# The order of TensorE work by the size of the weight loads in an attention and feed-forward kernel

## The chip, the cores and the metric

The kernel runs on one core of one Trainium2 chip. The metric is the device time of one execution in microseconds (us). The kernel before the change takes 1217.96 us (median of three runs, 1214.26 to 1219.36).

## What is computed

Eight batches of eight heads of causal attention over 576 tokens of width 64, with a forget gate whose cumulated logarithm is added to the scores, and then a layer norm, a two-layer feed-forward block (512 to 2048 to 512) and a residual over the 4608 tokens:

```
scores = scale * np.matmul(q, k.transpose(0, 1, 3, 2))
cum = np.cumsum(np.log(np.clip(f, 0.0001, 1.0)), axis=-1)
scores = np.where(causal, -1e9, scores + cum[:, :, :, None] - cum[:, :, None, :])
attn = np.exp(scores - np.max(scores, axis=-1, keepdims=True))
attn = attn / (np.sum(attn, axis=-1, keepdims=True) + 1e-09)
x = np.matmul(attn, v)            # heads side by side: (8, 576, 512)
xn = (x - mu) / np.sqrt(var + 1e-06) * g_ln
out = x + np.maximum(xn @ w_ch1, 0.0) @ w_ch2
```

All of it is held to the accuracy of float32, though TensorE multiplies in a shorter format: a factor is split into a high part and a low part (a rounded copy and what the rounding lost), and the products of high by high, high by low and low by high are added up in PSUM.

## The kernel before, in words

**Slots.** The program is one stream of slots, numbered u. A slot stands for a pair (head n, row tile t), t = 1 to 4; 64 heads make 256 slots. A row tile has 128 queries, and the tile t needs the keys up to its diagonal: 192, 320, 448 and 576. The first 64 queries of a head are a small tile t = 0 of 64 queries by 64 keys, done in the slot of t = 1. Keys are cut into one block of 64 and blocks of 128.

**What a slot issues.** The string in the table ORDERS that is valid for the slot says in which order its pieces are issued; each letter is one piece. The strings change at u = 37 and u = 66. The letters that matter here:

- Q: scores of (n, t) on TensorE (qk_mm, lines 374, 376 and 377), a product of the high parts and one of the rest;
- S, e, B: the softmax of the same tile: minimum and mask on VectorE (L409), exponential on ScalarE (L420), the reciprocal on VectorE (L425, L426), the scaling on GpSimd (L427) and a DMA on SyncE's queue (L440) that copies the tile p to pw, a tile with TensorE's short type;
- t: transposes on TensorE of the tile that was made two slots earlier (transpose_unit, recorded at L446 for pw and L448 for p);
- h, l: their results are copied from PSUM by ScalarE (L504, the high part ph) and subtracted by VectorE (L509, the low part pl);
- A: the product with v (av_unit, L543), in slots of t = 1 and t = 3 alone, for the rows transposed in the slots before;
- F, a: its result is copied by ScalarE (L579) and added by VectorE (L590), and sent to memory (L592);
- M, r, m: twelve products of the feed-forward's first layer (L622 to L624) and the two parts of their result, by ScalarE (L630) and VectorE (L635);
- N: six products of the second layer (L644 to L646) for the result of the slot before.

So after u = 66 a slot is a few small products of the attention followed by twelve products of 256 columns and six of 512 columns of the feed-forward. Each engine executes what it is given in the order of issue. The PSUM banks of all these pieces are one ring of six (tag b).

**Two kinds of heads.** Heads 0 to 15 (h.full) are computed in float32 throughout, while the feed-forward's weights are prepared; their products with v (L518) write the two halves of the columns to different partitions. Heads 16 to 63 use the short type and the split parts.

**Stationary and moving.** A product on TensorE first loads its stationary operand (PEld in the profile: LDWEIGHTS), and then streams the moving one. In the profile's form "128\*64 128x256" the stationary operand has 128 rows and 64 columns, and 256 columns are streamed. A transpose has the data as its stationary operand and streams the 128 columns of an identity; the transpose of a 64-key block has a stationary operand of 64 columns, all others have 128. The scores of tile t = 0 have 64 columns, as have the low parts of the product with v (pl times the high half of v); the high parts have 128.

Of the kernel before, what the change touches and what calls it, by code (L numbers as in the profile page):

```python
# [17 lines left out]
P = 128  # L18
# [30 lines left out]
ORDERS = [  # L49
    (0, "WwQsSthAeMrgFBmlLNPaRf"),  # L50
    (37, "WwQSstAMhPelgNFrfmBDLRba"),
    (66, "QSAFteahBlMPrmNbRLD"),
]


# [1 line left out]
def attn_moe(ctx: ExitStack, tc: tile.TileContext, qk, v, f, g, w1, w2, out):  # L57
# [385 lines left out]
    def tr(out_, in_):  # L443
        m = in_.shape[0]
        if in_.dtype == F32R:
            nc.tensor.transpose(out_.bitcast(F32R), in_, identr[:m, :m])  # L446
        else:
            nc.tensor.transpose(out_, in_, ident[:m, :m])  # L448
# [5 lines left out]
    def transpose_unit(h, t):  # L454
        n = f"{h.n}"
        pt = h.p[t][0]
        work_ = []
        if t <= 2:
            if t == 1:
                if h.full:  # L460
                    h.ph1 = padded_keys("ph1", 704, S1)
                else:
                    h.ph1 = work.tile([P, 704], F32R, tag="ph1", bufs=1, name=f"ph1_{n}")
                h.pl1 = None if h.full else pools["late"].tile([P, 384], F32R, tag="pl1", bufs=1, name=f"pl1_{n}")
            ph = h.ph1
            pl = ph if h.full else h.pl1
            tp = bank(f"tr{n}_{t}")
            if t == 1:
                tr(tp[0:64, 0:128], h.p[0][0])
                tr(tp[0:64, 64:192], pt[:, 0:64])  # L470
                tr(tp[:, 192:320], pt[:, 64:192])
                work_.append((tp[0:64, 0:192], ph[0:64, 0:192], ph[64:128, 0:192]))
                work_.append((tp[:, 192:320], ph[:, 320:448], pl[:, 0:128]))
            else:
                tr(tp[0:64, 0:128], pt[:, 0:64])
                tr(tp[:, 128:256], pt[:, 64:192])
                tr(tp[:, 256:384], pt[:, 192:320])
                work_.append((tp[0:64, 0:128], ph[0:64, 192:320], ph[64:128, 192:320]))
                work_.append((tp[:, 128:384], ph[:, 448:704], pl[:, 128:384]))
        else:  # L480
            if t == 3:
                if h.full:
                    h.ph2 = padded_keys("ph2", 9 * P, S - S1)
                else:
                    h.ph2 = work.tile([P, 9 * P], F32R, tag="ph2", bufs=1, name=f"ph2_{n}")
                h.pl2 = None if h.full else pools["late"].tile([P, 7 * P], F32R, tag="pl2", bufs=1, name=f"pl2_{n}")
            c = 0 if t == 3 else P
            ph = h.ph2[:, : 8 * P].rearrange("p (k c) -> p k c", k=4)[:, :, c : c + P]
            pl = None if h.full else h.pl2[:, : 6 * P].rearrange("p (k c) -> p k c", k=3)[:, :, c : c + P]
            tp = bank(f"tr{n}_{t}").rearrange("p (k c) -> p k c", k=4)  # L490
            tr(tp[0:64, 0, :], pt[:, 0:64])
            for k in range(1, 4):
                tr(tp[:, k, :], pt[:, 64 + P * (k - 1) : 64 + P * k])
            work_.append((tp[0:64, 0, :], ph[0:64, 0, :], ph[64:128, 0, :]))
            work_.append((tp[:, 1:4, :], ph[:, 1:4, :], pl))
            if t == 4:
                tp = bank(f"tr{n}_4b")[:, :P]
                tr(tp, pt[:, 64 + 3 * P : 64 + 4 * P])
                work_.append((tp, h.ph2[:, 8 * P :], None if h.full else h.pl2[:, 6 * P :]))
        h.parts = work_  # L500

    def transposed_hi(h, t):
# [8 lines left out]
    def av_unit(h, t):  # L511
        po = bank(f"o{h.n}_{t}")

        if h.full:

            def fac(cols, k, mv, first=False):
                half = slice(0, 64) if cols.start < SPLIT[t] else slice(64, P)
                mm(po[half, cols], h.vr[:, k], mv, start=first, stop=True, skip_group_check=True)  # L518

            if t == 2:  # L520
                ph = h.ph1
                for k, c0, q0 in ((0, 0, 0), (1, 320, 64)):
                    fac(slice(q0, 192), k, ph[:, c0 : c0 + 192 - q0], k == 0)
                    fac(slice(192, 320), k, ph[:, c0 + 192 - q0 : c0 + 320 - q0], k == 0)
                fac(slice(192, 320), 2, ph[:, 576:704])
                h.o = (po, S1, 0)
            else:
                ph = h.ph2
                for k in range(4):
                    for i in range(2):  # L530
                        c0 = 256 * k + P * i
                        fac(slice(P * i, P * i + P), k, ph[:, c0 : c0 + P], k == 0)
                fac(slice(128, 256), 4, ph[:, 8 * P :])
                h.o = (po, S - S1, S1)
            return

        vv = h.vv

        def both(k):
            return vv[:, k].rearrange("p a d -> p (a d)")  # L540

        def acc(o, st, mv, first=False):
            mm(o, st, mv, start=first, stop=True, skip_group_check=True)  # L543

        if t == 2:
            ph, pl, w, c0 = h.ph1, h.pl1, S1, 0
            acc(po[:, 0:320], both(0), ph[:, 0:320], True)
            acc(po[:, 64:320], both(1), ph[:, 320:576])
            acc(po[:, 192:320], both(2), ph[:, 576:704])
            acc(po[0:64, 64:320], vv[:, 1, 0, :], pl[:, 0:256])  # L550
            acc(po[0:64, 192:320], vv[:, 2, 0, :], pl[:, 256:384])
        else:
            ph, pl, w, c0 = h.ph2, h.pl2, S - S1, S1
            for k in range(4):
                acc(po[:, 0:256], both(k), ph[:, 256 * k : 256 * k + 256], k == 0)
            acc(po[:, 128:256], both(4), ph[:, 8 * P :])
            for k in range(1, 4):
                acc(po[0:64, 0:256], vv[:, k, 0, :], pl[:, 256 * (k - 1) : 256 * k])
            acc(po[0:64, 128:256], vv[:, 4, 0, :], pl[:, 6 * P :])
        h.o = (po, w, c0)  # L560

    xs_tile = {}
# [246 lines left out]
    for u, slot in enumerate(slots):  # L809
# [4 lines left out]
        if slot is not None:  # L814
            n, t = slot
            h = hd[n]
# [2 lines left out]
            av = hd[before(LAG + 1)[0]]  # L819
        want = moe.can(wp.ready()) and u >= FIRST_MOE  # L820

        def piece(c):
            tu = before(LAG)
            if c == "t" and tu is not None:
                transpose_unit(hd[tu[0]], tu[1])
            elif c == "h" and tu is not None:
                transposed_hi(hd[tu[0]], tu[1])
            elif c == "l" and tu is not None:
                transposed_lo(hd[tu[0]])
            elif c == "Q" and slot is not None:  # L830
                if t == 1:
                    qk_mm(h, 0)
                qk_mm(h, t)
            elif c == "A" and av is not None:
                av_unit(av, before(LAG + 1)[1])
            elif c == "S" and slot is not None:
                if t == 1:
                    softmax_a(h, 0)
                softmax_a(h, t)
            elif c == "e" and slot is not None:  # L840
                if t == 1:
                    softmax_e(h, 0)
                softmax_e(h, t)
            elif c in FILL:
                wp.fill(FILL[c])
            elif c == "s":
                wp.sums()
                if u == LAG:
                    busy(WARM[2])
            elif c == "F" and av is not None:  # L850
                finish(av)
            elif c == "a" and av is not None:
                finish_add(av)
            elif c == "r" and want:
                moe.first_high()
            elif c == "R":
                moe.limit = min(NCHUNK, max(0, u - LAG - 1) // (4 * H) * S // C)
                moe.rest()
            elif c == "b":
                rows_stats(moe.cur)  # L860
            elif c == "L":
                run_later(RSTD)
            elif c == "M" and want:
                moe.first()
            elif c == "B" and slot is not None:
                if t == 1:
                    softmax_b(h, 0)
                softmax_b(h, t)
            elif c == "m" and want:
                moe.first_low()  # L870
            elif c == "W":
                due = 1 + min(u, W_CHANGE) / W_SLOTS + max(0, u - W_CHANGE) * W_TICKS
                while not wp.done() and wp.tick_no <= due:
                    wp.tick()
            elif c == "N":
                moe.second()
            elif c == "P":
                prep()
            elif c == "D":
                next_raw()  # L880
# [81 lines left out]
```

## Time and profile before

| what | value |
|---|---|
| median of three runs | 1217.96 us (1214.26 to 1219.36) |
| the profiled execution's own time | 1217.98 us |
| its span, first to last instruction | 1216.1 us |
| transposes of pw, 128 columns (L446), 432 | mean record 240 ns |
| transposes of pw, 64 columns (L446), 240 | mean record 226 ns |
| product with v, low part, 256 moving columns (L543), 192 | mean record 279 ns |
| weight load of 128 columns for a product of the feed-forward (L622) | mean record 191 ns |
| weight load of 128 columns for a transpose (L446) | mean record 141 ns |
| weight load of 64 columns for a transpose (L446) | mean record 111 ns |

A record of a matmul or a weight load is longer than the time until the next one starts, since they are pipelined. So durations can't be added up here; what can be added up are the distances between the starts of successive records.

### The profile page before, as it was taken

Reading aid. Unit: us, or ns where it says so; the run is one execution under the profiler, and the core shown is the slowest. Engines: PE = TensorE matmul, PEld = TensorE weight load, DVE = VectorE, ACT = ScalarE, POOL = GpSimd, SP = SyncE. Lnnn points to the kernel's source line nnn. Section 1 sums busy time; section 2 is a strip of 40 time slices with the busy share of each in tenths; the row PEclk is TensorE's granted clock in tenths of the full one; section 3 lists DMA queues with packets and bytes.
Section 4 is the critical chain, followed back from the end, with each engine's and each line's share of the span. In section 5 each row is a group of like instructions: output and inputs, shape, how many; then the busy total and the mean of one; then the engine's idle time right before and its main releaser. Section 6 shows DMA issues by size and latency. Waiting matters only on the chain.

```text
span 1216.1 us, 25716 instructions
## 1 busy us (share of the span) xinstructions
PE 1190.1 (98%) x8368; PEld 1068.3 (88%) x8368; DVE 757.0 (62%) x2664; ACT 619.3 (51%) x1936; POOL 452.6 (37%) x768
## 2 busy tenths in 40 slices
PE   8888998999999999999999999999999999999998
PEld 6557887899999989999999999999999999999997
DVE  6777683477777767777767676767677752222122
ACT  6886574555555555555555555556555541112111
POOL 3543344454444434454534344445444410000000
PEclk9998998999999999999999999999999999999999
DMA  6454452243434344434344444434444421111100
GB/s 192 142 153 151 127 148 63 87 133 131 139 125 143 123 141 131 146 129 135 124 129 141 129 135 131 143 120 139 132 132 131 128 86 41 31 36 39 31 26 27
DMA packets 127541, 139.00 MB, mean 114 GB/s; under 512 B 32432, under 2 KB 100016, under 8 KB 127408
## 3 DMA queue, kind: packets, MB, share of 16 engines
q1 hardware_dynamic: 127408, 137.36, 36.6%
q8 instruction: 67, 1.10, 0.4%
q14 instruction: 66, 0.54, 0.1%
HBM read 79.61 MB, written 19.17 MB: 81 GB/s over the span
## 4 chain that ended last, share of the span: by engine, by line
PE 91%; DVE 3%; ACT 2%; DMA 1%; issue 1%; POOL 1%; SPq 0%; DVEq 0%; ACTq 0%; POOLq 0%
PE h L622 12%; PE h L624 11%; PE h L623 11%; PE acc L644 11%; PE acc L645 11%; PE acc L646 11%; PE o L543 6%; PE tr L446 4%; PE s L376 3%; PE s L377 3%; PE s L374 2%; PE o L518 2%; PE tr L448 1%; ACT p L420 1%; DVE p L409 1%
## 5 line engine op out<-in xcount | busy, mean ns | idle before, releaser
L427 POOL TENSOR_SCALAR p<-p,st 64x64 f32<-64x64 f32 (+4 forms) x320 | 169.9, 532 | 511.5 <-ACT ph L504 232.4
L622 PE MATMUL h<-x,w1h 128*128 128x256 f32 x1152 | 342.3, 297 | 0.4 <-DVE st L409 0.4
L624 PE MATMUL h<-x,w1l 128*128 128x256 f32 x1152 | 326.8, 284 | 0.0
L623 PE MATMUL h<-x,w1h 128*128 128x256 f32 x1152 | 326.3, 283 | 0.0
L420 ACT ACTIVATE p<-p,st 64x64 f32<-64x64 f32 (+4 forms) x320 | 179.2, 561 | 210.6 <-DVE st L409 206.0
L635 DVE SCALAR_TENSOR_TENSOR hh<-h,hh 128x256 fp32r<-128x256 f32 x288 | 120.5, 418 | 194.4 <-ACT hh L630 192.0
L644 PE MATMUL acc<-w2h,hh 128*128 128x512 f32 x576 | 228.4, 397 | 0.0
L645 PE MATMUL acc<-w2l,hh 128*128 128x512 f32 x576 | 227.8, 396 | 0.0
L646 PE MATMUL acc<-w2h,hh 128*128 128x512 f32 x576 | 225.5, 391 | 0.0
L622 PEld LDWEIGHTS h<-x,w1h 128*128 128x128 f32 x1152 | 219.6, 191 | 5.3 <-issue 0.9
L623 PEld LDWEIGHTS h<-x,w1h 128*128 128x128 f32 x1152 | 220.6, 192 | 2.5
L624 PEld LDWEIGHTS h<-x,w1l 128*128 128x128 f32 x1152 | 220.3, 191 | 0.0
L630 ACT ACTIVATE hh<-h 128x256 fp32r<-128x256 f32 x288 | 109.9, 381 | 184.5 <-PE h L624 184.2
L409 DVE CUSTOM_DVE_ANT_0 p<-s,mask 64x64 f32<-64x64 f32 (+4 forms) x320 | 132.2, 421 | 26.4 <-PE s L377 17.7
L646 PEld LDWEIGHTS acc<-w2h,hh 128*128 128x128 f32 x576 | 108.5, 188 | 24.7
L425 DVE TENSOR_SCALAR st<-st 128x1 f32<-128x1 f32 (+1 forms) x320 | 47.7, 149 | 120.2 <-ACT p L420 117.2
L644 PEld LDWEIGHTS acc<-w2h,hh 128*128 128x128 f32 x576 | 109.5, 190 | 14.0 <-ACT ph_full L504 0.2
L645 PEld LDWEIGHTS acc<-w2l,hh 128*128 128x128 f32 x576 | 109.5, 190 | 11.7
L504 ACT CAST ph<-tr 64x128 fp32r<-64x128 f32 (+4 forms) x384 | 107.2, 328 | 3.6 <-PE tr L446 1.3
L579 ACT COPY ot<-o 64x320 f32<-64x320 f32 x96 | 38.0, 396 | 125.5 <-PE tr L446 63.7
L509 DVE TENSOR_TENSOR pl<-tr,ph 128x128 fp32r<-128x128 f32 x192 | 88.0, 458 | 4.3
L377 PE MATMUL s<-kl,xq 66*128 66x288 f32 (+4 forms) x288 | 83.2, 297 | 0.0
(89 smaller groups left out, 1888.7 us busy)
## 6 DMA issues: line engine op xcount, KB each, us to landing
raw<-in_qk_dram SPq DMA_DIRECT2D x96, 288.0 KB
wr<-in_w_dram SPq DMA_DIRECT2D x32, 512.0 KB
pw<-p SPq DMA_DIRECT2D x48, 288.0 KB
pw<-p SPq DMA_DIRECT2D x48, 224.0 KB
vr<-in_v_dram SPq DMA_DIRECT2D x64, 160.0 KB
out_dram<-xt SPq DMA_DIRECT2D x36, 256.0 KB
pw<-p SPq DMA_DIRECT2D x48, 160.0 KB
xa<-xs SPq DMA_DIRECT2D x32, 160.0 KB
```

The costliest lines, as they stand in the source:

```text
L377: mm(sp, xq, kl, start=False, stop=True)
L409: nc.vector.tensor_tensor_reduce(out=pt[:m, a:z], in0=sp, in1=mask[:m, off + a : off + z], scale=-SCALE, scalar=3.0e38 if i == 0 else st[: ...
L420: nc.scalar.activation(pt[:m, :w], pt[:m, :w], AF.Exp, bias=st[:m, i : i + 1], scale=-1.0, accum_out=st[:m, 2:3])
L427: nc.gpsimd.tensor_scalar(out=pt[:m, :w], in0=pt[:m, :w], scalar1=st[:m, 3:4], scalar2=1.0, op0=ALU.mult, op1=ALU.mult)
L622: mm(ph, w1h[:, k, fs], c.x[k][:, 0, :], start=(k == 0), stop=False)
L623: mm(ph, w1h[:, k, fs], c.x[k][:, 1, :], start=False, stop=False)
L624: mm(ph, w1l[:, k, fs], c.x[k][:, 0, :], start=False, stop=(k == KT - 1))
L630: nc.scalar.activation(h[:, 0, :], c.ph, AF.Relu)
L635: nc.vector.scalar_tensor_tensor(out=h[:, 1, :], in0=ph, scalar=0.0, in1=h[:, 0, :].bitcast(F32), op0=ALU.max, op1=ALU.subtract)
L644: mm(c.acc[i], h[:, 0, ts_], w2h[:, j, :], start=(j == 0), stop=False)
L645: mm(c.acc[i], h[:, 0, ts_], w2l[:, j, :], start=False, stop=False)
L646: mm(c.acc[i], h[:, 1, ts_], w2h[:, j, :], start=False, stop=(j == FT - 1))
```

## The change

The instructions are the same, and the data. Their order changes in four ways:

1. In every row of transposes, the transpose of the 64-key block (for t = 1 also that of the tile t = 0) is issued last.
2. From u = 66 on, the transposes t stand ahead of the product with v, A. In the same string the exponential e and the reciprocal and scaling B now stand ahead of F, a.
3. In the product with v of heads 16 to 63, the low part of 128 moving columns is issued ahead of those of 256.
4. In slots of t = 1 of heads 16 to 63, the tile t = 1 comes ahead of the tile t = 0 in Q, S, e and B.

```
 ORDERS = [
     (0, "WwQsSthAeMrgFBmlLNPaRf"),
     (37, "WwQSstAMhPelgNFrfmBDLRba"),
-    (66, "QSAFteahBlMPrmNbRLD"),
+    (66, "QStAeBFahlMPrmNbRLD"),
 ]
...
             if t == 1:
+                tr(tp[:, 192:320], pt[:, 64:192])
                 tr(tp[0:64, 0:128], h.p[0][0])
                 tr(tp[0:64, 64:192], pt[:, 0:64])
-                tr(tp[:, 192:320], pt[:, 64:192])
...
             else:
-                tr(tp[0:64, 0:128], pt[:, 0:64])
                 tr(tp[:, 128:256], pt[:, 64:192])
                 tr(tp[:, 256:384], pt[:, 192:320])
+                tr(tp[0:64, 0:128], pt[:, 0:64])
...
-            tr(tp[0:64, 0, :], pt[:, 0:64])
             for k in range(1, 4):
                 tr(tp[:, k, :], pt[:, 64 + P * (k - 1) : 64 + P * k])
...
             if t == 4:
-                tp = bank(f"tr{n}_4b")[:, :P]
-                tr(tp, pt[:, 64 + 3 * P : 64 + 4 * P])
...
+                tb = bank(f"tr{n}_4b")[:, :P]
+                tr(tb, pt[:, 64 + 3 * P : 64 + 4 * P])
...
+            tr(tp[0:64, 0, :], pt[:, 0:64])
...
             acc(po[:, 192:320], both(2), ph[:, 576:704])
+            acc(po[0:64, 192:320], vv[:, 2, 0, :], pl[:, 256:384])
             acc(po[0:64, 64:320], vv[:, 1, 0, :], pl[:, 0:256])
-            acc(po[0:64, 192:320], vv[:, 2, 0, :], pl[:, 256:384])
...
             acc(po[:, 128:256], both(4), ph[:, 8 * P :])
+            acc(po[0:64, 128:256], vv[:, 4, 0, :], pl[:, 6 * P :])
             for k in range(1, 4):
                 acc(po[0:64, 0:256], vv[:, k, 0, :], pl[:, 256 * (k - 1) : 256 * k])
-            acc(po[0:64, 128:256], vv[:, 4, 0, :], pl[:, 6 * P :])
...
+        def tiles(h, t):
+            if t > 1:
+                return [t]
+            return [0, 1] if h.full else [1, 0]
...
             elif c == "Q" and slot is not None:
-                if t == 1:
-                    qk_mm(h, 0)
-                qk_mm(h, t)
+                for i in tiles(h, t):
+                    qk_mm(h, i)
```

The pieces S, e and B are changed as Q is.

The first place is TensorE in the slot of t = 1 of head 37, from its scores to the first product of the feed-forward (s: scores, o: product with v, tr: transposes, h: feed-forward). Before:

```order
L376 MATMUL s_0_0_8083<-hi_7951 64x128
L377 MATMUL s_0_0_8083<-kl_7952,xq_2933 64x128
L376 MATMUL s_1_0_8086<-hi_7951 128x192
L377 MATMUL s_1_0_8086<-kl_7952,xq_2933 128x192
L543 MATMUL o_2_8094<-ph_36_7985,vv_8019 128x320
L543 MATMUL o_2_8094<-ph_36_7985,vv_8019 128x256
L543 MATMUL o_2_8094<-ph_36_7985,vv_8019 128x128
L543 MATMUL o_2_8094<-pl_36_7986,vv_8019 64x256
L543 MATMUL o_2_8094<-pl_36_7986,vv_8019 64x128
L446 MATMUL tr_3_8105<-identr,pw_3_7999 64x128
L446 MATMUL tr_3_8105<-identr,pw_3_7999 128x128 x3
L622 MATMUL h_8_8126<-x_0_7148,w1h 128x256
```

And with the change, at the same place on TensorE:

```order
L376 MATMUL s_1_0_8083<-hi_7951 128x192
L377 MATMUL s_1_0_8083<-kl_7952,xq_2933 128x192
L376 MATMUL s_0_0_8086<-hi_7951 64x128
L377 MATMUL s_0_0_8086<-kl_7952,xq_2933 64x128
L446 MATMUL tr_3_8096<-identr,pw_3_7993 128x128 x3
L446 MATMUL tr_3_8096<-identr,pw_3_7993 64x128
L543 MATMUL o_2_8101<-ph_36_7973,vv_8019 128x320
L543 MATMUL o_2_8101<-ph_36_7973,vv_8019 128x256
L543 MATMUL o_2_8101<-ph_36_7973,vv_8019 128x128
L543 MATMUL o_2_8101<-pl_36_7974,vv_8019 64x128
L543 MATMUL o_2_8101<-pl_36_7974,vv_8019 64x256
L622 MATMUL h_8_8126<-x_0_7148,w1h 128x256
```

The first number of a row's size is here that of the stationary operand's columns. The pair of scores of 64 columns has moved behind that of 128, the transposes ahead of the product, and in both groups the one of 64 columns and 128 moving ones has changed its place.

The second place is TensorE in the slot of t = 3 of the same head. Before:

```order
L377 MATMUL s_3_0_8214<-kl_7952,xq_2933 128x448
L543 MATMUL o_4_8220<-ph_36_8103,vv_8019 128x256 x4
L543 MATMUL o_4_8220<-ph_36_8103,vv_8019 128x128
L543 MATMUL o_4_8220<-pl_36_8104,vv_8019 64x256 x3
L543 MATMUL o_4_8220<-pl_36_8104,vv_8019 64x128
L446 MATMUL tr_1_8235<-identr,pw_2893 64x128
L446 MATMUL tr_1_8235<-identr,pw_1_8122 64x128
L446 MATMUL tr_1_8235<-identr,pw_1_8122 128x128
```

And with the change:

```order
L377 MATMUL s_3_0_8214<-kl_7952,xq_2933 128x448
L446 MATMUL tr_1_8222<-identr,pw_1_8112 128x128
L446 MATMUL tr_1_8222<-identr,pw_2898 64x128
L446 MATMUL tr_1_8222<-identr,pw_1_8112 64x128
L543 MATMUL o_4_8226<-ph_36_8094,vv_8019 128x256 x4
L543 MATMUL o_4_8226<-ph_36_8094,vv_8019 128x128
L543 MATMUL o_4_8226<-pl_36_8095,vv_8019 64x128
L543 MATMUL o_4_8226<-pl_36_8095,vv_8019 64x256 x3
```

The row of transposes has moved ahead of the product, its 128-column one first, and the product now ends with the low parts of 256 moving columns.

The third place is ScalarE in the slot of t = 1 of head 37 (p: exponentials, ot: the copied product, ph: high parts of the transposes, hh: feed-forward). Before:

```order
L579 COPY ot_0_8101<-o_2_8094 64x320
L420 ACTIVATE p_1_177,st_0_8089<-p_1_177,st_0_8089 64x64
L420 ACTIVATE p_1_8091,st_1_8092<-p_1_8091,st_1_8092 128x192
L504 CAST ph_36_8103<-tr_3_8105 64x128
L504 CAST ph_36_8103<-tr_3_8105 128x3x128
L630 ACTIVATE hh_8_8139<-h_8_8126 128x256
```

And with the change:

```order
L420 ACTIVATE p_1_8089,st_1_8090<-p_1_8089,st_1_8090 128x192
L420 ACTIVATE p_1_177,st_0_8092<-p_1_177,st_0_8092 64x64
L579 COPY ot_0_8119<-o_2_8101 64x320
L504 CAST ph_36_8094<-tr_3_8096 64x128
L504 CAST ph_36_8094<-tr_3_8096 128x3x128
L630 ACTIVATE hh_8_8139<-h_8_8126 128x256
```

The copy of the product has moved behind the exponentials and stands right ahead of the copies of the transposes and of the feed-forward's result, which are behind it on the engine.

More of the change, by code (lines that the diff above doesn't have):

```diff
@@ L51 @@
     (37, "WwQSstAMhPelgNFrfmBDLRba"),
-    (66, "QSAFteahBlMPrmNbRLD"),
+    (66, "QStAeBFahlMPrmNbRLD"),
 ]
@@ L468, in transpose_unit @@
             if t == 1:
+                tr(tp[:, 192:320], pt[:, 64:192])
                 tr(tp[0:64, 0:128], h.p[0][0])
                 tr(tp[0:64, 64:192], pt[:, 0:64])
-                tr(tp[:, 192:320], pt[:, 64:192])
                 work_.append((tp[0:64, 0:192], ph[0:64, 0:192], ph[64:128, 0:192]))
@@ L474, in transpose_unit @@
             else:
-                tr(tp[0:64, 0:128], pt[:, 0:64])
                 tr(tp[:, 128:256], pt[:, 64:192])
                 tr(tp[:, 256:384], pt[:, 192:320])
+                tr(tp[0:64, 0:128], pt[:, 0:64])
                 work_.append((tp[0:64, 0:128], ph[0:64, 192:320], ph[64:128, 192:320]))
@@ L490, in transpose_unit @@
             tp = bank(f"tr{n}_{t}").rearrange("p (k c) -> p k c", k=4)
-            tr(tp[0:64, 0, :], pt[:, 0:64])
             for k in range(1, 4):
@@ L496, in transpose_unit @@
             if t == 4:
-                tp = bank(f"tr{n}_4b")[:, :P]
-                tr(tp, pt[:, 64 + 3 * P : 64 + 4 * P])
-                work_.append((tp, h.ph2[:, 8 * P :], None if h.full else h.pl2[:, 6 * P :]))
+                tb = bank(f"tr{n}_4b")[:, :P]
+                tr(tb, pt[:, 64 + 3 * P : 64 + 4 * P])
+                work_.append((tb, h.ph2[:, 8 * P :], None if h.full else h.pl2[:, 6 * P :]))
+            tr(tp[0:64, 0, :], pt[:, 0:64])
         h.parts = work_
@@ L549, in av_unit @@
             acc(po[:, 192:320], both(2), ph[:, 576:704])
+            acc(po[0:64, 192:320], vv[:, 2, 0, :], pl[:, 256:384])
             acc(po[0:64, 64:320], vv[:, 1, 0, :], pl[:, 0:256])
-            acc(po[0:64, 192:320], vv[:, 2, 0, :], pl[:, 256:384])
         else:
@@ L556, in av_unit @@
             acc(po[:, 128:256], both(4), ph[:, 8 * P :])
+            acc(po[0:64, 128:256], vv[:, 4, 0, :], pl[:, 6 * P :])
             for k in range(1, 4):
                 acc(po[0:64, 0:256], vv[:, k, 0, :], pl[:, 256 * (k - 1) : 256 * k])
-            acc(po[0:64, 128:256], vv[:, 4, 0, :], pl[:, 6 * P :])
         h.o = (po, w, c0)
@@ L820, in attn_moe, with tiles @@
         want = moe.can(wp.ready()) and u >= FIRST_MOE
+        def tiles(h, t):
+            if t > 1:
+                return [t]
+            return [0, 1] if h.full else [1, 0]
         def piece(c):
@@ L830, in piece @@
             elif c == "Q" and slot is not None:
-                if t == 1:
-                    qk_mm(h, 0)
-                qk_mm(h, t)
+                for i in tiles(h, t):
+                    qk_mm(h, i)
             elif c == "A" and av is not None:
@@ L836, in piece @@
             elif c == "S" and slot is not None:
-                if t == 1:
-                    softmax_a(h, 0)
-                softmax_a(h, t)
+                for i in tiles(h, t):
+                    softmax_a(h, i)
             elif c == "e" and slot is not None:
-                if t == 1:
-                    softmax_e(h, 0)
-                softmax_e(h, t)
+                for i in tiles(h, t):
+                    softmax_e(h, i)
             elif c in FILL:
@@ L865, in piece @@
             elif c == "B" and slot is not None:
-                if t == 1:
-                    softmax_b(h, 0)
-                softmax_b(h, t)
+                for i in tiles(h, t):
+                    softmax_b(h, i)
             elif c == "m" and want:
```

## The prediction

> **What bounds the kernel now.** I read the page's busy shares and its chain first, then the windows by stage, then the waits of TensorE alone.
>
> ```profile
> span 1216.1 us, 25716 instructions
> PE 1190.1 (98%) x8368; PEld 1068.3 (88%) x8368; DVE 757.0 (62%) x2664; ACT 619.3 (51%) x1936; POOL 452.6 (37%) x768
> ...
> PEclk9998998999999999999999999999999999999999
> ...
> PE 91%; DVE 3%; ACT 2%; DMA 1%; issue 1%; POOL 1%; SPq 0%; DVEq 0%; ACTq 0%; POOLq 0%
> ```
>
> TensorE carries 91% of the chain that ended last. Where it does not is told by the windows; the first two columns of times are PE and PEld:
>
> ```profile
> 0.00:120.00 120.00, 102.26 (x707) 76.08 (x708) 90.01 (x330) 89.78 (x277) 52.16 (x83) 0.96 0.55 160
> 120.00:240.00 120.00, 115.96 (x819) 98.72 (x818) 69.69 (x251) 68.69 (x212) 48.52 (x73) 0.97 0.35 105
> 240.00:1030.00 790.00, 789.76 (x5675) 728.56 (x5675) 553.12 (x1984) 429.26 (x1365) 341.07 (x557) 1.00 0.41 127
> ```
>
> From 240 to 1030 us, where heads 16 to 63 are computed, PE is busy for 789.76 of 790 us at the full clock (1.00). The waits of PE and PEld from 250 us to the end are these, and no others:
>
> ```profile
> PE o L543 <- DVE ph L509: 0.2, 1, 0.2
> ...
> PEld o L543 <- DVE ph L509: 0.6, 1, 0.6
> PEld tr L446 <- DVE hh L635: 0.3, 1, 0.3
> PEld tr L446 <- DMA pw<-p: 0.2, 1, 0.2
> PEld o L543 <- issue: 0.2, 1, 0.2
> ```
>
> So in this stage nothing waits for data, and its length is the sum of the steps from one matmul to the next. The change adds and removes no instruction; it can only alter these steps, or bring in waits.
>
> **What a step costs.** One slot of t = 1, weight loads alone (start, length of the record, stationary form, count):
>
> ```profile
> 703.25 0.13 PEld L377 LDWEIGHTS s<-kl,xq 66*64 66x64 f32 x1
> 703.31 0.19 PEld L376 LDWEIGHTS s<-hi 128*128 128x128 f32 x1
> 703.42 0.19 PEld L377 LDWEIGHTS s<-kl,xq 66*128 66x128 f32 x1
> 703.54 0.45 PEld L543 LDWEIGHTS o<-ph,vv 128*128 128x128 f32 x3
> 703.92 0.20 PEld L543 LDWEIGHTS o<-pl,vv 128*64 128x64 f32 x2
> 704.09 0.37 PEld L446 LDWEIGHTS tr<-identr,pw 128*64 128x64 f32 x4
> 704.41 0.19 PEld L622 LDWEIGHTS h<-x,w1h 128*128 128x128 f32 x1
> 704.52 0.19 PEld L623 LDWEIGHTS h<-x,w1h 128*128 128x128 f32 x1
> 704.64 0.19 PEld L624 LDWEIGHTS h<-x,w1l 128*128 128x128 f32 x1
> ```
>
> A load starts when the load before it is through and its operand has been taken over, that is, when the matmul before begins to stream. The distance between two loads is therefore the longer of two things: the streaming of the running matmul, and the load of the next. Streaming 256 columns takes 0.12 (704.52 to 704.64). Behind 128 moving columns it depends on what is loaded: 0.06 for the next load of 64 columns (703.25 to 703.31), but 0.11 for one of 128 (703.31 to 703.42, after the 64-column scores). The row of four transposes is one load of 64 and three of 128 columns, 704.09 to 704.41: 0.32, so a 128-column load for a transpose takes (0.32 - 0.06) / 3 = 0.087. The same slot type t = 3:
>
> ```profile
> 711.28 0.19 PEld L377 LDWEIGHTS s<-kl,xq 66*128 66x128 f32 x1
> 711.48 0.76 PEld L543 LDWEIGHTS o<-ph,vv 128*128 128x128 f32 x5
> 712.17 0.42 PEld L543 LDWEIGHTS o<-pl,vv 128*64 128x64 f32 x4
> 712.58 0.11 PEld L446 LDWEIGHTS tr<-identr,pw 128*64 128x64 f32 x1
> 712.70 0.14 PEld L446 LDWEIGHTS tr<-identr,pw 128*128 128x128 f32 x1
> 712.78 0.19 PEld L622 LDWEIGHTS h<-x,w1h 128*128 128x128 f32 x1
> 712.89 0.19 PEld L623 LDWEIGHTS h<-x,w1h 128*128 128x128 f32 x1
> ```
>
> Two 64-column transposes take 0.12 (712.58 to 712.70), then 0.08 for the 128-column one, then 0.11 for the first load of the feed-forward. A load is free if it hides behind a long stream, and a 64-column one hides behind anything.
>
> **The change part by part, in heads 16 to 63.**
>
> *64-key blocks last.* The first load of a row of transposes hides behind what streams before it. Before, that was the 64-column load, and all 128-column loads stood open; now one 128-column load is hidden and the 64-column one costs 0.06 behind 128 columns. Per row: 0.087 - 0.06 = 0.027 gained. In slots of t = 2 and t = 4, which have no product with v, that is the whole change.
>
> *t = 3.* After the change, from the last scores: scores 0.20, transposes 0.06 + 0.06, then 0.11 for the product's first load behind the last transpose, four products of 256 columns 0.48 (0.12 each, as 711.48 to 712.17 is 0.69 with the scores' 0.20 or 0.21), then 0.06 (128 columns, 64-column load next), 0.06 (the short low part first), and three low parts 0.35 (712.17 to 712.58 is 0.41, less 0.06), the last hiding the feed-forward's load. Sum 1.38. Before, 711.48 to 712.89 is 1.41. Gain 0.03, which is again the row of transposes: moving it ahead of A exchanges one open 0.11 for another, and the low part's order exchanges 0.06 for 0.06.
>
> *t = 1.* After: scores of 192 columns 0.11 (a 128-column load next), then the second one with a 64-column load next. That step is not in the trace; it lies between 0.06 (128 columns streamed) and 0.12 (256), and I take 0.09, halfway as 192 is. Then 0.06 between the 64-column scores, 3 x 0.087 and 0.06 for the transposes, 0.11 to the product; its high parts 0.15 + 0.12 (703.54 to 703.92 is 0.38, less 0.11 for the first), 0.06, low parts 0.06 + 0.12. Sum 1.20; before, 703.25 to 704.52 is 1.27. Gain 0.07.
>
> Per head 0.07 + 3 x 0.027 = 0.15; 48 heads, less the two slots before u = 66: **7.2 us**.
>
> *Order of the softmax, of F and of a.* Costed at nothing, as other engines have room in this stage (DVE 553, ACT 429, POOL 341 of 790 us). What covers it: F waits for the product, which now ends later, and the copies h, r and VectorE's l, m are queued behind F and a. The rows of the slot above:
>
> ```profile
> 704.40 0.42 ACT L579 COPY ot<-o 64x320 f32<-64x320 f32 x1 [1.12 <-PE o L543]
> 705.75 0.64 ACT L504 CAST ph<-tr 64x128 fp32r<-64x128 f32 x2
> ...
> 707.19 0.41 DVE L635 SCALAR_TENSOR_TENSOR hh<-h,hh 128x256 fp32r<-128x256 f32 x1
> ...
> 710.35 0.39 PE L646 MATMUL acc<-w2h,hh 128*128 128x512 f32 x1
> ...
> 698.66 0.47 SPq L440 DMA_DIRECT2D pw<-p  x1
> ```
>
> The casts start when the exponentials end (705.75), and would now wait for F first: 0.42 later, and so would hh's low part, done at 707.60. TensorE wants it at 710.35, 2.75 later. The transposes are wanted earlier: in t = 1 after 0.11 + 0.09 + 0.06 = 0.26 instead of 0.84 (703.25 to 704.09), 0.58 sooner; the tile was sent at 698.66, 5.4 ahead of its use at 704.09, and will have 4.8. On SyncE's queue the send of pw now stands ahead of the one of xs, so it is not later. If the cover were gone, TensorE would wait by the difference in each such slot.
>
> *Heads 0 to 15.* Their transposes are in float32:
>
> ```profile
> 142.53 0.14 PEld L448 LDWEIGHTS tr_4b<-identr,p 128*128 128x128 f32 x1
> 142.65 0.19 PEld L622 LDWEIGHTS h<-x,w1h 128*128 128x128 f32 x1
> ...
> PEld tr L448 <- POOL p L427: 16.2, 25, 1.6
> ...
> ACT ph_full L504 <- PE tr L448: 1.5, 2, 1.0
> ```
>
> A float32 transpose streams for 0.11 (142.53 to 142.65), so no load is hidden or opened by the order: nothing gained. From 10 to 110 us (the two waits) TensorE itself waits for the tiles. In rows of t = 1 it now starts with the tile that GpSimd scales last, so up to two transposes that could go ahead follow instead: at most 0.11 a head, 16 heads, 1.8; and ScalarE's first cast waits for the last transpose, 0.33 in 2 places: 0.7. Between 0 and 2.5 lost; a quarter of the 25 waits belong to t = 1, so I take 0.5.
>
> **Sum.** 1217.98 (the profiled execution's own time; its span is 1216.1, and the median is 1217.96, the same) - 7.2 + 0.5 = **1211.3 us**. With the unknown step at 0.06 or 0.12 (48 x 0.03 = 1.4) and the early loss at its ends it is 1209.4 to 1214.7.
>
> **Rivals.**
>
> *New waits take half.* At the 18 changes of chunk, extra copies stand on ScalarE and VectorE, and the only waits in the list above are 0.2 to 0.6 long; one of them is for pw, another for hh, so the cover is thin there. At 0.2 for each of 18: 3.6, time 1214.9. For it: 0.42 more delay, tiles wanted 0.58 sooner. Against: a cover of 2.75 and 4.8 in the usual slot.
>
> *Each switch between 64 and 128 columns empties the array.* Per head there were 10 such switches and now there are 14 (two more in each slot with A), 192 more. The rows are those of the low parts of 256 columns (busy time, mean of one record in ns) and of an early head:
>
> ```profile
> L543 PE MATMUL o<-pl,vv 128*64 128x256 f32 x192 | 38.1, 279 | 0.0
> ...
> 137.25 0.52 PEld L448 LDWEIGHTS tr<-identr,p 128*64 128x64 f32 x4
> 137.94 0.20 PEld L518 LDWEIGHTS o<-ph_full,vr 128*64 128x64 f32 x4 [0.17 <-issue]
> ```
>
> The price of an emptied array is what a record is longer than its step: 0.28 - 0.12 = 0.16. 192 x 0.16 = 30.7 gives 1242, **slower**. It decides from 35 ns a switch for no gain, and from 67 ns for over 0.5% slower. For it: in the early heads some 0.2 passes between the transposes and the product. Against it: in heads 16 on, 64 to 128 columns takes the load's own 0.11 (703.31) or 0.087, no more. By the Trainium skill, "TensorEngine Tiling (Array Packing)", section Key Properties, changing the tiling mode drains TensorE; if 64 columns were such a mode, that would be this rival's 1242, and by the rows of the late heads it is not.
>
> *The loads do not run under the streams, and order is indifferent:* 1218.0. Against it: 256 columns with a 128-column load take 0.12, not 0.11 + 0.12. By the Trainium skill, "TensorE: Matmul & The Clock Gate", section The mechanism, loads overlap matmuls in flight only when the row group differs, which would give this 1218.0; the rows at 704.52 and 704.64 disagree.
>
> *The early gap closes.* If the 0.2 at 137.94 stems from the switch of columns, a 64-column transpose in front of the product halves it: 32 products x 0.1 = 3.2, time 1208.1. Against: the late heads show no such cost.
>
> **How the numbers follow.** Forecast 0.65, new waits 0.18, emptied array 0.04, indifferent 0.06, early gap 0.07. The range 1208 to 1216 leaves out the emptied array, the indifferent order and a little more. A measurement of this kernel can tell about 0.5% from no change, here 1211.9, so the forecast stands just beyond it: 0.48 of its 0.65, with the early gap, is faster by over 0.5% (0.55); 0.17 and the waits and the indifferent order are within (0.41); the emptied array is slower (0.04).
>
> **What would show it.** Right: loads of TensorE in t = 1 from the first scores to the feed-forward's second load within 1.20 and no new wait of PE beyond 1 us in total after 250 us. Wrong: steps above 0.12 behind the low parts of 256 columns (the emptied array), waits of tr for pw or of acc for hh (the cover), or a start of the late heads that is more than 2.5 later than before.

## The result, and the profile after

The change makes the kernel **slower by 0.7%**: 1226.0 us (median of 7 runs, 1221.83 to 1229.61) beside 1216.97 us before on the same chip (7 runs, 1213.68 to 1219.36), ratio 1.0072, 95% interval 1.0047 to 1.0098. The forecast was 1211.3 us, range 1208 to 1216. The profiled execution took 1227.63 us, its span is 1225.8 us.

The page of the kernel after, the rows that answer to those of before (span, busy time by engine, clock by slice):

```profile
span 1225.8 us, 25669 instructions
PE 1190.0 (97%) x8368; PEld 1065.6 (87%) x8368; DVE 759.2 (62%) x2664; ACT 622.4 (51%) x1936; POOL 454.8 (37%) x768
...
PEclk9998998999999999999999999999999999999999
```

The three windows by stage (length, busy time of PE, PEld, DVE, ACT, POOL, clock, DMA share, GB/s), and all waits of PE and of PEld from 250 us to the end (total us, times, longest):

```profile
0.00:120.00 120.00, 101.55 (x710) 75.54 (x711) 90.36 (x330) 90.11 (x278) 52.20 (x83) 0.97 0.55 160
120.00:240.00 120.00, 115.59 (x816) 98.72 (x815) 69.89 (x252) 68.53 (x211) 48.89 (x73) 0.97 0.36 105
240.00:1030.00 790.00, 781.02 (x5614) 717.65 (x5613) 551.11 (x1974) 429.57 (x1358) 340.10 (x543) 1.00 0.41 127
```

```profile
PE o L543 <- DVE ph L509: 4.1, 11, 0.9
PE o L543 <- DVE pl L509: 2.6, 5, 0.5
PE tr L446 <- DMA pw<-p: 2.0, 6, 0.5
```

```profile
PEld o L543 <- DVE ph L509: 5.6, 13, 0.5
PEld o L543 <- issue: 4.2, 6, 1.0
PEld tr L446 <- issue: 1.9, 4, 0.7
PEld tr L446 <- DMA pw<-p: 1.0, 1, 1.0
PEld tr L446 <- DVE hh L635: 0.9, 2, 0.5
PEld tr L446 <- DVE pl L509: 0.4, 1, 0.4
```

The clock is the same, and the first two windows differ by less than 1 us of PE. In the third, PE now idles for 9.0 of 790 us where it idled for 0.24: the stage that waited for nothing has waits, most of them at the product with v for the parts ph and pl that VectorE writes (6.7 of PE's 8.7 us above), the rest at transposes.

To part steps from waits I went through the weight loads of heads 16 to 63. The "late stage" runs from 2.6 us ahead of the first load of L376 to the last one. From the distance of each load to the next I took the longer of the running matmul's streaming and the next load's time, by the prices of the prediction; what was left, where it was over 0.04 us, is summed as "waits". One of these waits can stand at the transposes of the last head, behind the late stage; the table lists it beside the sum that it is part of, and "steps" is the late stage without the other waits. From each kernel's profiled execution, in us:

| kernel | late stage begins | late stage | waits (number) | of these behind it | steps | time behind it | span |
|---|---|---|---|---|---|---|---|
| before | 220.7 | 766.1 | 1.7 (8) | 0.1 | 764.5 | 229.3 | 1216.1 |
| after | 220.4 | 775.5 | 18.4 (46) | 0.9 | 758.0 | 229.9 | 1225.8 |

So the steps did become shorter, by 6.5 us, where 7.2 was forecast; with each kind of step at its median over all fourteen profiles the two orders differ by 7.0. Inside the late stage the waits are 17.5 instead of 1.6 us. These new 15.9 us took the gain and 9.4 more, and 9.4 is what the whole span gained, within 0.3.

### The profile page after: what moved, and what is told of

The parts are those of the page before. It is cut to its first block, busy times and chain, and to the rows that moved or that the text cites. A ratio compares the mean times of both kernels' runs of the same rounds, so it can differ in the third digit from the quotient of the medians.

```text
span 1225.8 us, 25669 instructions
## 1 busy us (share of the span) xinstructions
PE 1190.0 (97%) x8368; PEld 1065.6 (87%) x8368; DVE 759.2 (62%) x2664; ACT 622.4 (51%) x1936; POOL 454.8 (37%) x768
## 5 line engine op out<-in xcount | busy, mean ns | idle before, releaser
L622 PE MATMUL h<-x,w1h 128*128 128x256 f32 x1152 | 334.9, 291 | 0.4 <-DVE st L409 0.4
L623 PE MATMUL h<-x,w1h 128*128 128x256 f32 x1152 | 326.4, 283 | 0.0
L409 DVE CUSTOM_DVE_ANT_0 p<-s,mask 64x64 f32<-64x64 f32 (+4 forms) x320 | 130.6, 422 | 17.6 <-PE s L377 5.0
L350 POOL TENSOR_TENSOR hi<-raw,hi 64x576 fp32r<-64x576 f32 x48 | 77.7, 1619 | 20.9 <-POOL p L427 18.6
L446 PE MATMUL tr<-identr,pw 128*128 128x128 f32 (+1 forms) x672 | 82.4, 234 | 2.1 <-DMA pw<-p 2.0
```

Of the source, the lines that this page charges most:

```text
L409: nc.vector.tensor_tensor_reduce(out=pt[:m, a:z], in0=sp, in1=mask[:m, off + a : off + z], scale=-SCALE, scalar=3.0e38 if i == 0 else st[: ...
L622: mm(ph, w1h[:, k, fs], c.x[k][:, 0, :], start=(k == 0), stop=False)
L623: mm(ph, w1h[:, k, fs], c.x[k][:, 1, :], start=False, stop=False)
```

## Where the new waits lie

Of the 46 waits, 13 (6.2 us) are at the first high part of the product with v in slots of t = 3; 12 of them about 64 us apart, which is 16 slots, a chunk: 281.3, 345.2, 409.2 and so on. Another 15 (2.8 us) are at its first low part, mostly in the same slots. 7 (4.6 us) are at the product in slots of t = 1, and 9 (3.7 us) at transposes of the tile t = 4, waiting for pw (what delayed pw there was not followed). The last two are the one of 0.9 behind the late stage, at 1003.7, and one of 0.15 at a float32 product of head 15. Here is VectorE after, around the one at 409.2 (start, length, instruction, the idle time before it and its releaser):

```profile
401.33 0.97 DVE L607 TENSOR_TENSOR x<-xr,x 128x256 fp32r<-128x256 f32 x2
402.22 0.35 DVE L409 CUSTOM_DVE_ANT_0 p<-s,mask 128x192 f32<-128x192 f32 x1
...
403.19 0.15 DVE L425 TENSOR_SCALAR st<-st 128x1 f32<-128x1 f32 x1 [0.48 <-ACT p L420]
...
403.97 0.48 DVE L590 TENSOR_TENSOR xs<-o,ot 64x320 f32<-64x320 f32 x1
404.63 0.28 DVE L509 TENSOR_TENSOR ph<-tr,ph 64x128 fp32r<-64x128 f32 x1 [0.18 <-ACT ph L504]
404.92 0.56 DVE L509 TENSOR_TENSOR pl<-tr,ph 128x384 fp32r<-128x384 f32 x1
405.40 0.42 DVE L635 SCALAR_TENSOR_TENSOR hh<-h,hh 128x256 fp32r<-128x256 f32 x1
405.73 1.40 DVE L721 SCALAR_TENSOR_TENSOR xt<-acc,rs,xt 128x512 f32<-128x512 f32 x2
407.05 0.48 DVE L409 CUSTOM_DVE_ANT_0 p<-s,mask 128x320 f32<-128x320 f32 x1
```

ScalarE in the same slot, and TensorE two slots later, at the product that waits:

```profile
402.61 0.46 ACT L420 ACTIVATE p<-p,st 128x192 f32<-128x192 f32 x1 [1.42 <-DVE st L409]
403.06 0.33 ACT L420 ACTIVATE p<-p,st 64x64 f32<-64x64 f32 x1
403.51 0.42 ACT L579 COPY ot<-o 64x320 f32<-64x320 f32 x1
...
409.17 0.80 PE L543 MATMUL o<-ph,vv 128*128 128x256 f32 x5 [0.31 <-DVE ph L509]
```

And VectorE before, same head and slot:

```profile
401.25 0.21 DVE L409 CUSTOM_DVE_ANT_0 p<-s,mask 64x64 f32<-64x64 f32 x1
...
401.67 0.48 DVE L590 TENSOR_TENSOR xs<-o,ot 64x320 f32<-64x320 f32 x1
402.07 0.13 DVE L425 TENSOR_SCALAR st<-st 64x1 f32<-64x1 f32 x1
...
403.85 0.41 DVE L635 SCALAR_TENSOR_TENSOR hh<-h,hh 128x256 fp32r<-128x256 f32 x1
```

Before, VectorE went from the minima (L409) straight to the addition of the product's copy (L590, the piece a), and the exponential ran on ScalarE meanwhile. After, VectorE has nothing between the minima and the reciprocal and idles for 0.48; then the addition stands behind the copy F (403.51), and F behind both exponentials. From the first minimum to the end of hh's low part it takes 405.82 - 402.22 = 3.60 instead of 404.26 - 401.25 = 3.01. That is a **relay**: VectorE, ScalarE, VectorE, with F and a now at its end instead of inside it. In a usual slot VectorE has room for it. At a chunk's change it also has the feed-forward's extra pieces (L607, L721), and the parts for the product of the next slots come up to 0.55 late. All waits of VectorE for the exponential from 240 to 1030 us, before and then after:

```profile
DVE st L425 <- ACT p L420: 94.7, 141, 0.9
```

```profile
DVE st L425 <- ACT p L420: 142.3, 188, 1.0
```

That is 47 more such waits in 48 heads.

## The experiments

All kernels compute the whole result; only order and engines differ. "After" and "before" in an edit say which kernel it starts from. The profiled executions enter the late stage between 216.8 and 221.8 us, though their code up to there hardly differs, so spans scatter by some us, and waits and steps tell kernels apart more sharply than spans do:

| kernel | time, us | ratio to before (95%) | late stage | waits (number) | of these behind it | steps |
|---|---|---|---|---|---|---|
| e1_copy_first | 1212.1 | 0.9963 (0.9945 to 0.9981) | 763.0 | 5.5 (22) | 0.9 | 758.4 |
| e2_softmax_first_only | 1222.53 | 1.0055 (1.0035 to 1.0075) | 771.9 | 9.0 (24) | 0.4 | 763.3 |
| e3_tile_order_back | 1221.24 | 1.0044 (1.0024 to 1.0064) | 771.1 | 13.9 (40) | 1.6 | 758.8 |
| e4_copy_first_add_last | 1273.79 | 1.0467 (1.0437 to 1.0498) | 820.9 | 63.7 (88) | 0 | 757.2 |
| e5_old_string | 1212.57 | 0.9973 (0.9953 to 0.9992) | 764.3 | 6.0 (28) | 0.2 | 758.5 |
| e6_old_string_old_tiles | 1212.02 | 0.9955 (0.9936 to 0.9975) | 761.7 | 2.4 (9) | 0 | 759.3 |
| e7_copy_first_old_tiles | 1213.57 | 0.9959 (0.9941 to 0.9978) | 761.7 | 3.2 (13) | 0.5 | 759.0 |
| e8_low_part_on_pool | 1210.12 | 0.9939 (0.9914 to 0.9963) | 760.4 | 3.3 (14) | 1.4 | 758.5 |
| e9_before_pool | 1214.15 | 0.9991 (0.9980 to 1.0001) | 766.0 | 2.1 (4) | 0.7 | 764.6 |
| e10_copy_first_pool | 1209.9 | 0.9955 (0.9942 to 0.9967) | 762.3 | 4.8 (18) | 0.5 | 758.0 |
| e11_add_last_pool | 1252.56 | 1.0307 (1.0286 to 1.0329) | 805.4 | 47.2 (66) | 0 | 758.2 |
| e12_cast_on_act | 1213.88 | 0.9984 (0.9962 to 1.0005) | 762.6 | 4.2 (21) | 0 | 758.3 |

### The order of the softmax alone: e1 and e2

e1 is after with F ahead of e, and a between e and B, as before:

```diff
-    (66, "QStAeBFahlMPrmNbRLD"),
+    (66, "QStAFeahBlMPrmNbRLD"),
```

> The changed kernel with one thing put back: the copy and the addition of the product with v (F, a) stand again ahead of the exponential and of the reciprocal (e, a, then h, B, l), while the transposes stay ahead of the product. Theory relay: the waits of TensorE in the changed kernel (18.4 us after 223 us, summed over steps more than 40 ns too long) come from VectorE and ScalarE handing work to each other without overlap in slots with A: VectorE finishes the softmax's first part, idles for the exponential, and only then does the addition, for which ScalarE copies only behind the exponential. Then here the waits fall below 5 us and the steps' gain of some 7 us stays: 1209 to 1214 us, ratio to before 0.992 to 0.998. Rival late product: F waits for a product that now ends 0.4 us later in the slot, and all behind it is late whatever the order on ScalarE and VectorE; then over 10 us of waits stay, 1220 us or more. Rival tile order: the waits come from tile 1 standing ahead of tile 0; then they stay as well.

e2 is before with the new order of the softmax and nothing else:

```diff
-    (66, "QSAFteahBlMPrmNbRLD"),
+    (66, "QSAteBFahlMPrmNbRLD"),
```

> The kernel before with one part of the change: e and B ahead of F and a, with the product still ahead of the transposes, and every other order as before. Theory relay: nothing is gained on TensorE's steps and waits come in: more than 8 us of them after 223 us, 1226 to 1236 us, ratio 1.006 to 1.015. Rival late product, and rival tile order: no new waits, 1215 to 1220 us, ratio 0.998 to 1.002.

The waits of e1 are 5.5 instead of 18.4 (a little above the 5 expected) at nearly the same steps (758.4 and 758.0), and the kernel is faster than before; e2's are 9.0 instead of 1.7, and the kernel is slower by 0.55%, a little less than expected. So this part of the change alone costs more than measurement can miss, from either side: 7.3 us of waits on top of before, 12.9 on top of the other parts. The rival of the late product falls with e1, where the product is as late as in after. By their order e2's steps are those of before, yet they come out 1.2 lower: no finer than that can steps and waits be told apart here. VectorE's waits for the exponential go with it. From 240 to 1030 us in e1, then in e2:

```profile
DVE st L425 <- ACT p L420: 98.2, 141, 1.0
```

```profile
DVE st L425 <- ACT p L420: 127.7, 186, 0.9
```

### The order of the two tiles: e3, and the pairs e5 to e7

e3 is after with the tile t = 0 first in all heads:

```diff
-            return [0, 1] if h.full else [1, 0]
+            return [0, 1]
```

> The changed kernel with the tile t = 0 ahead of t = 1 again in Q, S, e and B. Theory relay: the waits stay at 12 us or more, and the steps lose what the tile order gained in slots of t = 1, some 0.04 us a head, 2 us: 1224 to 1230 us, ratio 1.005 to 1.011. Rival tile order: the waits fall below 5 us and the time to 1211 to 1215 us. Rival late product: as the theory relay.

e5 is after with the string of before; e6 is e5 with e3's edit, e7 is e1 with e3's edit:

```diff
-    (66, "QStAeBFahlMPrmNbRLD"),
+    (66, "QSAFteahBlMPrmNbRLD"),
```

> The changed kernel with the whole string of u = 66 put back (product ahead of the transposes, F ahead of e, a ahead of B), but with the 64-key blocks last, the short low part first and tile 1 ahead of tile 0. Theory relay: ScalarE and VectorE stand as in the kernel before, so the waits of TensorE after 223 us fall to about those of before (1.7 us; I say below 4), less than in the first run with the copy first (5.5). The steps lose the 128-column load of the product behind the 64-column scores, 0.02 us a head against the changed kernel: 1 us. So 1209 to 1212 us, ratio 0.992 to 0.996. Rival tile order: waits of 5 us or more stay, 1213 us or more. Rival: the gain of the steps needs the transposes ahead of the product; then 1215 or more.

> As the run with the old string, and also the tile t = 0 ahead of t = 1 again: only the order inside the rows of transposes and of the low parts is left of the change. By the steps of the trace this is worth 4 x 0.027 us a head, 5 us in all: 1210 to 1213 us, ratio 0.993 to 0.998, waits as before (below 3 us). If the order inside the rows were worth nothing and the gain came from the transposes ahead of the product: 1215 to 1219.

> The run with the copy first (transposes ahead of the product, F and a ahead of e and B), with the tile t = 0 ahead of t = 1 again. In the changed kernel that took the waits from 18.4 to 13.9 us and the steps did not get longer. Theory relay: here it has less to act on: waits of 2 to 5 us against 5.5, 1209 to 1213 us, ratio 0.992 to 0.997. Rival, tile order does nothing by itself: waits 5 to 6 us, 1211 to 1214 us.

Tile t = 1 first costs waits in each pair; inside the late stage they are 17.5 against 12.3 (after and e3), 5.8 against 2.4 (e5 and e6), 4.6 against 2.7 (e1 and e7). e3, expected at 1224 us or more, took 1221.24. The rows above suggest why: the first exponential starts 0.39 behind the first minimum (402.61 - 402.22), where with the small tile it was 0.25 (401.50 - 401.25), by this row of ScalarE before:

```profile
401.50 0.35 ACT L420 ACTIVATE p<-p,st 64x64 f32<-64x64 f32 x1
```

With F and a behind the exponentials that is added to VectorE's wait: 142.3 us of it after, and 129.8 in e3. Where a fills the wait (e5, e6) both orders have 95.1, so e5's waits are not explained by it. The steps that it should shorten gain 0.8, 0.8 and 0.6 us (758.8 to 758.0, 759.3 to 758.5, 759.0 to 758.4), where 2 was expected: it costs more than it brings. e5's waits, expected under 4, were 6.0 because the tile order is still in it. e6 and e7 differ by the transposes ahead of the product: 0.3 less in steps, 0.3 more in waits, and the late stage is as long in both, so that part is worth nothing. What is left in e6, the 64-key transposes last and the short low part first, carries 5.2 of the 6.5 us (764.5 to 759.3) nearly without a wait.

### The copy first, the addition last: e4

If the copy's place alone made after slow, F ahead of e with a left behind B would do:

```diff
-    (66, "QStAeBFahlMPrmNbRLD"),
+    (66, "QStAFeBahlMPrmNbRLD"),
```

> The changed kernel with the copy F ahead of the exponential on ScalarE, but the addition a still behind the reciprocal on VectorE (F, e, B, a, h, l): this splits the relay between its two engines. If ScalarE's order is what costs (the copy behind the exponential, so that the addition, and all behind it, waits twice), the waits fall below 5 us: 1209 to 1214 us. If VectorE's order is what costs (it idles for the exponential with the addition behind it), over 8 us of waits stay: 1219 us or more. I expect a part of each, with VectorE's the larger: 6 to 12 us of waits, 1215 to 1222 us, ratio 0.998 to 1.004.

A miss by far: 4.7% slower, 63.7 us of waits, 49.3 of them in 46 waits of 1.07 at the product in slots of t = 1, one for each head. One row of the groups stands out (total busy us, mean ns of one), first e1, then e4; xq is a rounded copy of the queries for the next head:

```profile
L349 DVE CAST xq<-raw 64x576 fp32r<-64x576 f32 x48 | 21.2, 442 | 0.0
```

```profile
L349 DVE CAST xq<-raw 64x576 fp32r<-64x576 f32 x48 | 76.1, 1586 | 0.0
```

The same instruction on the same operands takes 0.44 us in one kernel and 1.59 in the other. On the timeline GpSimd's subtraction L350 is beside it, in e1 begun 0.17 after the cast, in e4 0.16 ahead of it:

```profile
408.27 0.44 DVE L349 CAST xq<-raw 64x576 fp32r<-64x576 f32 x1
...
408.44 1.56 POOL L350 TENSOR_TENSOR hi<-raw,hi 64x576 fp32r<-64x576 f32 x1
```

```profile
406.46 1.43 POOL L350 TENSOR_TENSOR hi<-raw,hi 64x576 fp32r<-64x576 f32 x1
...
406.62 1.59 DVE L349 CAST xq<-raw 64x576 fp32r<-64x576 f32 x1
408.13 0.47 DVE L356 CAST vv<-vr 128x320 fp32r<-128x320 f32 x1
```

46 of the 48 casts are over 1 us long in e4, one in after, none in before and e1. By the Trainium skill, "SBUF — State Buffer", section Who interferes with whom, VectorE and GpSimd share a pair of ports as an exclusive lock, and whoever issues first holds it for the whole instruction; casts are among the operations named there that can need it. The rows agree: the later one of the two is the longer (1.59 instead of 0.44, or 1.56 instead of 1.43). The excess, 1.59 - 0.44 = 1.15, is about the 1.07 of each wait. What was left was whether the cast is the cause or one more sign of VectorE being late. In after the lock is no rival to the relay: the means there and before are 0.467 and 0.447 us for the cast, 0.581 and 0.574 for VectorE's subtraction L607, 1.619 and 1.557 for GpSimd's L350, and VectorE's busy time from 240 to 1000 us is 543.05 and 545.02.

### Less work on VectorE: e8 to e11, and e12

If the relay hurts only where VectorE is crowded, taking chunk work off VectorE must help with the relay in place. In e8 (from after), e9 (from before), e10 (from e1) and e11 (from e4) the subtraction for the feed-forward's low part of x, 72 instructions of 0.58 us, goes to GpSimd:

```diff
-        nc.vector.tensor_tensor(out=x[:, 1, :], in0=xr, in1=x[:, 0, :].bitcast(F32), op=ALU.subtract)
+        nc.gpsimd.tensor_tensor(out=x[:, 1, :], in0=xr, in1=x[:, 0, :].bitcast(F32), op=ALU.subtract)
```

> The changed kernel, in which GpSimd computes the low part of the feed-forward's inputs (72 subtractions of 0.58 us, some of them at each change of chunk) in place of VectorE; nothing else is altered. Theory relay: the waits arise where VectorE, already late from the relay, also has the work of a chunk's change; with part of that gone they fall from 18.4 to 5 to 12 us: 1217 to 1223 us, ratio 1.000 to 1.005. Rival late product: the waits stay at 15 or more and the time at 1222 to 1228 us. GpSimd is busy for 43% of the late stage and has the tiles p in its queue; if it becomes the bound instead, waits of tr for pw appear.

> The control for the run with the low part on GpSimd: the kernel before, with that move alone and none of the new order. Its TensorE waits for 1.7 us after 223 us, so there is little to take away: ratio to before 0.997 to 1.002, 1213 to 1219 us, the sum of steps as before (761 to 762 us). If instead the gain of that run came from the move itself and not from the order with its waits taken away, this one is faster by 0.4% or more as well.

> The run with the copy first, and with the low part on GpSimd. Steps of 754 to 755 us as there; waits of TensorE from 5.5 to 1.5 to 3.5 us: 1208 to 1212 us, ratio 0.992 to 0.996, as fast as the changed kernel with the low part on GpSimd or a little faster. If the order of F and e still cost something with VectorE relieved, this one is faster than that by 0.2% or more.

> The slowest run (F, e on ScalarE, B ahead of a on VectorE: 63.7 us of waits), with the low part on GpSimd. There TensorE waited in 46 of 48 heads, not only at changes of chunk, so theory relay says that its chain from the scores through F, e, B, a, l to hh is too long for a slot by itself; taking chunk work away helps only part: 30 us of waits or more stay, 1235 us or more. If VectorE's work at the changes of chunk were needed for its waits as well, they fall below 15 us and the time below 1220.

In e8 the relay stays as it was, but TensorE's waits go. VectorE's waits for the exponential (240 to 1030 us), and all of PE's waits from 250 us on:

```profile
DVE st L425 <- ACT p L420: 142.3, 187, 1.1
```

```profile
PE tr L446 <- DMA pw<-p: 1.0, 1, 1.0
```

142.3 us as in after, yet 3.3 us of waits instead of 18.4, fewer than the 5 to 12 expected, at nearly after's steps (758.5 and 758.0). The wait for pw above, at 986.2, is behind the late stage; of after's 44 waits at products with v and transposes inside it none is left, those away from the chunks' changes included. e8 takes 1210.12 us, below the 1217 to 1223 expected, ratio 0.9939: it beats both kernels. The move is worth nothing to the kernel before (e9: 0.9991), which has hardly a wait to lose. In e10 it brings next to nothing: 4.8 instead of 5.5, a miss (1.5 to 3.5 expected), since GpSimd delivers x's low part later and 12 waits of 0.18 appear at the chunks' changes (in e8 12 of 0.14); at one of them GpSimd's second subtraction ends at 339.07 and the product that reads it starts at 339.12. With both, the softmax's new order costs nothing that could be told: the intervals of e8 and e10 overlap. In e11 most of e4's waits stay, as expected.

e12 is e4 with the cast on ScalarE:

```diff
-        nc.vector.tensor_copy(out=h.xq[0:64, :], in_=h.raw[0][0:64, :])
+        nc.scalar.copy(out=h.xq[0:64, :], in_=h.raw[0][0:64, :])
```

> The kernel of e4_copy_first_add_last (F ahead of e and B, a behind them), with the cast of the queries to xq (L349) moved from VectorE to ScalarE. Nothing is left out. Theory: e4's 63.7 us of new waits come for the most part from that cast, which takes 1.6 us on VectorE instead of 0.44 when GpSimd's subtraction L350 has begun ahead of it; on ScalarE (estimate 0.6 us, from its casts of the same size) nothing of the kind happens, and the waits of TensorE over 40 ns fall to 5 to 20 us, the late stage to 760 to 775, the time to 1212 to 1226. Rival: the place of a behind the exponential alone makes e4 slow, and the cast is only a sign of VectorE being late; then the waits stay above 40 us and the time above 1245.

The waits fall from 63.7 to 4.2 us, below the expected band, and the time to 1213.88. VectorE's waits for the exponential are no shorter than e4's 163.7, as the same order stands in both:

```profile
DVE st L425 <- ACT p L420: 174.3, 187, 1.8
```

So most of e4's loss was the cast behind GpSimd's subtraction: freeing VectorE of 21 us of casts that run unhindered (48 x 0.44) can hardly be it, since e11 freed it of 37 (72 x 0.52, their mean in e4) and kept 47.2 us of waits. That the cast is also off VectorE's queue does help e12, and the two shares were not told apart.

## Why the prediction was wrong, point by point

**Steps: right, a little less than forecast.** 7.2 us forecast, 6.5 measured. The slot of t = 1, weight loads alone, after:

```profile
400.51 0.19 PEld L377 LDWEIGHTS s<-kl,xq 66*128 66x128 f32 x1
400.62 0.14 PEld L376 LDWEIGHTS s<-hi 128*64 128x64 f32 x1
400.71 0.14 PEld L377 LDWEIGHTS s<-kl,xq 66*64 66x64 f32 x1
400.80 0.36 PEld L446 LDWEIGHTS tr<-identr,pw 128*128 128x128 f32 x4
401.11 0.45 PEld L543 LDWEIGHTS o<-ph,vv 128*128 128x128 f32 x3
401.48 0.19 PEld L543 LDWEIGHTS o<-pl,vv 128*64 128x64 f32 x2
401.60 0.19 PEld L622 LDWEIGHTS h<-x,w1h 128*128 128x128 f32 x1
401.71 0.19 PEld L623 LDWEIGHTS h<-x,w1h 128*128 128x128 f32 x1
```

From 400.51 to 401.71 it is 1.20, as summed. The step that no trace showed, 192 columns with a 64-column load next, is 0.09 (400.62 to 400.71), as taken. The next, between the two scores of 64 columns, is 0.09 where 0.06 was taken; the transposes' row, 0.31, gives a little of it back. Over all heads the median of this stretch is 1.208, and 1.265 before: 0.057 gained where 0.07 was forecast, 0.6 us in 48 heads. By parts the working fits less well: of the 3.4 us for slots of t = 1 (48 x 0.07), 1.3 is the row of transposes (48 x 0.027), and the other 2.1 should come from the tile order and the transposes ahead of the product. The runs show 0.6 to 0.8 and 0.3 for these, which the 1.2 us of doubt in the split leaves open.

**Heads 0 to 15: no loss seen.** The late stage begins at 220.4 instead of 220.7; 0.5 was taken, from a range of 0 to 2.5. The runs together begin it between 216.8 and 221.8, so one profile of each can't tell these apart. The loads' waits for GpSimd's tiles from 10 to 110 us are 17.3 us where they were 16.2.

**Order of the softmax, of F and of a: the step that failed.** It was "costed at nothing, as other engines have room in this stage", with a cover of 2.75 us for hh and 4.8 for pw. Both covers hold in the slot they were read from: after has no such wait from 671 to 728 us. Three things were not worked out. First, the addition a was counted as queued work, but not that it had filled VectorE's wait for the exponential; e2 shows that alone at 7.3 us of waits. Second, a share of 553 of 790 us is a mean: at the changes of chunk VectorE has no room, and there it shows (e8 against after). Third, the chain that became late, the casts ph and pl for the next product with v, was not among the two covers; 35 of the 46 waits are at the product.

**New waits take half: the right kind, far too small.** It had 18 places at 0.2, 3.6 us; it is 46 places with 0.40 in the mean (18.4 / 46). Of its 18 changes of chunk only 12 lie in the late stage. Its places were the changes of chunk, which is right for the 13 waits of t = 3 and the low parts with them; the product in t = 1 and the transposes of t = 4 add 8.3 us elsewhere.

**Each switch empties the array: refuted.** Behind the low parts of 256 columns the next load of 128 comes after 0.11 to 0.12 (401.60 to 401.71), the streaming alone. **Loads do not run under streams:** refuted by the 6.5 us of steps. **The early gap closes:** refuted. In heads 0 to 15 the distance from the last transpose's load to the product's first is 0.308 us (median of 31) in both kernels, though the last transpose has 128 columns before and 64 after.

## What to carry to other kernels

When an engine of 60 to 70% load waits for another in the middle of a chain, see what short work fills that wait now; moving it behind the wait lengthens the chain by its own time and by the wait, and it shows first where the engine is full, so the cover must be read in the fullest slots and for every consumer of the chain. An order that shortens TensorE's steps and one that feeds it are two changes: try them apart, since here the first was worth 6.5 us and the second cost 15.9. Where a reorder shifts a VectorE copy against a long GpSimd operation by as little as 0.3 us, compare the durations of unchanged instructions, not only the waits.

## What the runs showed of the hardware

That the relative start of two unchanged instructions decides so much was not expected: from 0.17 us ahead to 0.16 behind, a third of a microsecond, took the cast from 0.44 to 1.59 us, while GpSimd's subtraction went from 1.56 to 1.43. Nor that the profile counts it as work: VectorE's busy time from 240 to 1000 us, where e4 gets less done, is 553.53 us, and 538.92 in e1. The cast's row has no idle time before it (0.0); the loss appears as waits further on, at TensorE's products.
